# Nineteen seven-product blocks in place of eighteen, in another order, and two edits to the last block's tail

## The chip, the cores and the metric

The kernel runs on one core of a Trainium2 chip. A core has five engines that run side by side and meet through semaphores: TensorE (PE, matmuls, with its weight loads PEld), VectorE (DVE), ScalarE (ACT), GpSimd (POOL) and SyncE (SP). Each works through its own list of instructions in order. SP, ACT and POOL can also issue DMA transfers. The metric is the device time of one execution in microseconds, a median over runs.

## The reference

An input x of 8 x 4096 x 192 goes through a causal depthwise convolution over time with seven taps. Eight heads of 24 channels share a tap's weight, and the weights go through a softmax first. The result, as 32768 tokens of 192 channels, goes through a two-layer network: 192 to 2048, exact GELU, 2048 to 192.

```python
w = np.exp(weight - max); w = w / (w.sum(-1) + 1e-9)          # 8 heads x 7 taps
out = np.einsum('hk,bskhg->bshg', w, x_unf)                    # causal convolution
h = out.reshape(32768, 192) @ w_in                             # 192 -> 2048
g = 0.5 * h * (1 + erf(h / sqrt(2)))
return g @ w_out                                               # 2048 -> 192
```

## The kernel before

**Tiles.** The tokens are split in two halves of 16384, on 64 partitions each. A block n takes a run of tokens from both: blocks 0 to 5 take 256, blocks 6 to 34 take 512. While TensorE does the first product of block n, it does the second product of block n-1 in between.

**A block's way.** SP loads x into one of three buffers (`load`; a buffer is free when its last block is transposed). VectorE transposes it (`t`, line 1023). ScalarE writes the first tap as three scaled copies (`f0`, `f1`, `f2`, line 1157), VectorE adds the other six ("1" to "6", line 359; each tap waits for the one before; the sixth writes `xc`), POOL copies the six columns that overlap with the block before (`halo`). TensorE multiplies by w_in (line 1292, 48 rounds; a round is four 64x512 matmuls that run side by side), ScalarE applies GELU in 16 steps (line 1199) and writes `gT`, TensorE multiplies by w_out, the result is transposed into `osb` by VectorE and stored by SP (line 845, four DMAs a block).

**Two kinds of second product.** A plain block ("N") takes 48 rounds (line 1377) and three evacuations `ev.0` to `ev.2` by VectorE (line 477). A seven-product block (in `ST`) treats two of the three 64-channel thirds of the output as a 2x2 block product with seven products in place of eight, in Winograd's form: 44 rounds (line 1426). It pays in sums that other engines make of `gT`:

- `S1` in three parts (line 734) and `S3` in three parts: `S3.2` by VectorE (line 737), `S3.0` and `S3.1` by POOL as accumulating DMAs (line 691).
- `Dn` in two parts (line 740). Where the block before is plain, `Dn.0` is made by POOL instead, as a copying DMA (`cp`) and an accumulating one (lines 717, 721). Then `S4` in two parts (line 743).
- Four ScalarE copies out of PSUM, `p15`, `e`, `u`, `p3` (line 782); POOL moves u's result with two DMAs, `cu` and `cg` (line 686).
- VectorE's `k0` (line 790), which waits for the group P7 of the block's own matmuls and without which P4, later in the same block, can't start; `k3` (797), which waits for `cu`; `k4` (803), which waits for `cg` and for the block's last matmul; and three evacuations (line 815).

**The order.** It is written out by hand. `LIST[n]` is VectorE's order while it makes block n's convolution: a word `S1.0.8` is part 0 of S1 of block 8, `t9` is a transpose, a digit is a tap, `w` is one of ten preparations of the weights for the seven products, `evac` an evacuation of block 5. `SLOT[b]` tells before which GELU step of block b ScalarE does a first tap or a copy. `GLIST` is POOL's order. `AHEAD[n]` tells how many blocks SP has asked for before it stores block n-1. VectorE works about two blocks ahead of the GELU, so block m's sums stand in lists m+1 and m+2.

**The tail.** Block 34's second product runs alone, as 128x128 matmuls (line 1482) of four groups g of two banks h, 16 matmuls each. Group 0 of bank 0 waits for the GELU after every fourth. VectorE evacuates bank 0 of each group (line 449) and SP stores it, ScalarE evacuates bank 1 (line 451) and stores it (line 459). SP first stores all of block 33.

Of the kernel before, what the change touches and what calls it, by code (L numbers as in the profile page):

```python
# [11 lines left out]
def bass_lightweight_conv__then__act_gelu_exact_kernel(  # L12
# [24 lines left out]
    NB = len(WS)  # L37
# [16 lines left out]
    AHEAD = {4: 11, 5: 11, 7: 13, 8: 15, 9: 16, 10: 16, 11: 19, 12: 19, 13: 20, 14: 21, 15: 22, 16: 23, 17: 25, 18: 25, 19: 25, 22: 26, 23: 31, 24: 31, 25: 33, 26: 33, 27: 33, 28: 35, 29: 35}  # L54
# [20 lines left out]
    ST = [m for m in [8, 10, 11, 13, 14, 16, 17, 19, 20, 22, 24, 25, 27, 29, 30, 31, 32, 33] if m < M1]  # L75
    TYPE = {m: "S" if m in ST else "N" for m in range(-4, NB + 4)}
    LIST = {
        4: "t5 w.0.0 w.1.0 1 2 w.2.0 3 4 5 6",
        5: "t6 1 2 3 4 w.3.0 5 6",
        6: "w.4.0 t7 1 w.5.0 2 w.6.0 3 4 5 6",  # L80
        7: "t8 1 2 3 evac.0.5 w.7.0 4 5 6",
        8: "evac.1.5 t9 1 2 3 4 5 6",
        9: "ev.0.6 1 t10 2 ev.2.6 3 ev.1.6 4 5 w.8.0 6",
        10: "t11 1 2 S1.0.8 3 S1.1.8 ev.0.7 w.9.0 4 ev.1.7 S1.2.8 ev.2.7 Dn.1.8 S3.2.8 5 6",
        11: "S4.0.8 S4.1.8 k0.0.8 t12 1 2 3 ev.2.8 4 5 6",
        12: "t13 1 2 3 S1.0.10 4 ev.0.9 k4.0.8 k3.0.8 S1.1.10 5 ev.1.8 ev.0.8 ev.1.9 S1.2.10 S3.2.10 6",
        13: "Dn.1.10 S4.0.10 ev.2.9 1 S4.1.10 2 k0.0.10 3 4 S1.0.11 S1.1.11 Dn.0.11 ev.2.10 5 S1.2.11 Dn.1.11 S3.2.11 t14 6",
        14: "k4.0.10 t15 S4.0.11 S4.1.11 ev.0.10 k0.0.11 1 2 k3.0.10 3 ev.2.11 4 ev.1.10 5 6",
        15: "t16 1 2 S1.0.13 3 4 k3.0.11 ev.1.11 5 k4.0.11 S1.1.13 ev.0.12 ev.1.12 S1.2.13 ev.2.12 ev.0.11 Dn.1.13 S3.2.13 S4.0.13 S4.1.13 6",
        16: "t17 k0.0.13 1 S1.0.14 2 3 Dn.0.14 ev.2.13 S1.1.14 4 S1.2.14 S3.2.14 Dn.1.14 5 k4.0.13 ev.0.13 S4.0.14 S4.1.14 6",  # L90
        17: "k0.0.14 k3.0.13 t18 1 2 ev.2.14 3 4 ev.1.13 5 k4.0.14 6",
        18: "t19 ev.0.14 1 S1.0.16 2 ev.0.15 3 S1.1.16 4 k3.0.14 ev.1.15 ev.2.15 S1.2.16 ev.1.14 S3.2.16 Dn.1.16 5 S4.0.16 S4.1.16 6",
        19: "t20 k0.0.16 S1.0.17 1 2 ev.2.16 S1.1.17 3 4 S1.2.17 Dn.0.17 5 S3.2.17 k4.0.16 Dn.1.17 S4.0.17 S4.1.17 k0.0.17 k3.0.16 6",
        20: "1 t21 ev.2.17 ev.1.16 2 ev.0.16 3 4 5 6",
        21: "1 2 S1.0.19 t22 3 k4.0.17 ev.0.17 k3.0.17 ev.0.18 4 S1.1.19 S1.2.19 ev.1.18 S3.2.19 5 Dn.1.19 ev.2.18 6",
        22: "ev.1.17 S4.0.19 S4.1.19 k0.0.19 t23 1 S1.0.20 S1.1.20 ev.2.19 2 3 S1.2.20 4 S3.2.20 Dn.0.20 Dn.1.20 k4.0.19 S4.0.20 S4.1.20 k0.0.20 5 6",
        23: "1 t24 ev.2.20 k3.0.19 ev.0.19 ev.1.19 2 3 4 5 6",
        24: "S1.0.22 1 k3.0.20 ev.1.20 k4.0.20 ev.0.21 S1.1.22 t25 ev.0.20 2 ev.2.21 S1.2.22 ev.1.21 S4.0.22 Dn.1.22 S3.2.22 3 S4.1.22 4 k0.0.22 5 6",
        25: "t26 1 ev.2.22 2 3 4 5 6",
        26: "1 2 k4.0.22 t27 ev.0.23 3 ev.0.22 S1.0.24 4 S1.1.24 5 ev.1.23 S1.2.24 Dn.1.24 S3.2.24 k3.0.22 ev.2.23 ev.1.22 6",  # L100
        27: "S4.0.24 S4.1.24 k0.0.24 1 2 S1.0.25 Dn.0.25 S1.1.25 ev.2.24 3 4 S1.2.25 S3.2.25 t28 5 k4.0.24 Dn.1.25 S4.0.25 S4.1.25 k0.0.25 k3.0.24 6",
        28: "1 t29 2 ev.2.25 3 ev.0.24 ev.1.24 4 5 6",
        29: "1 2 S1.0.27 t30 3 S1.1.27 4 ev.0.26 k4.0.25 ev.1.26 S1.2.27 5 ev.2.26 k3.0.25 S3.2.27 ev.0.25 6",
        30: "ev.1.25 Dn.1.27 S4.0.27 S4.1.27 k0.0.27 t31 1 2 3 ev.2.27 4 5 6",
        31: "t32 1 k4.0.27 2 S1.0.29 3 4 5 ev.0.28 S1.1.29 k3.0.27 6",
        32: "S1.2.29 ev.2.28 ev.1.28 ev.1.27 S3.2.29 S4.0.29 ev.0.27 Dn.1.29 1 S4.1.29 k0.0.29 2 S1.0.30 3 t33 S1.1.30 ev.2.29 4 Dn.0.30 S1.2.30 S3.2.30 S4.0.30 5 Dn.1.30 k4.0.29 S4.1.30 k3.0.29 ev.1.29 k0.0.30 ev.0.29 6",
        33: "t34 S1.0.31 S1.1.31 1 ev.2.30 2 S1.2.31 Dn.0.31 Dn.1.31 S3.2.31 S4.0.31 S4.1.31 k4.0.30 3 4 k3.0.30 k0.0.31 5 6",
        34: "S1.0.32 S1.1.32 Dn.0.32 ev.2.31 1 ev.1.30 S1.2.32 S4.0.32 S3.2.32 ev.0.30 Dn.1.32 k4.0.31 2 S4.1.32 3 k0.0.32 4 5 S1.0.33 6",
        35: "ev.2.32 S1.1.33 S1.2.33 k3.0.31 Dn.0.33 ev.0.31 S4.0.33 S3.2.33 ev.1.31 k4.0.32 ev.0.32 k3.0.32 ev.1.32 Dn.1.33 S4.1.33 k0.0.33 ev.2.33 k4.0.33 ev.0.33 k3.0.33 ev.1.33",
# [3 lines left out]
        3: "0:f0.5 4:f1.5 5:f2.5 7:f0.6",  # L113
        4: "2:f1.6 5:f2.6 6:f0.7",
        5: "2:f1.7 6:f2.7",
        7: "0:f0.8 3:f1.8 3:f2.8 8:f0.9 9:f1.9 12:f2.9",
        8: "1:f0.10 5:f1.10 6:f2.10 10:f0.11 10:f1.11",
        9: "5:f2.11 7:p15.8 11:f0.12 14:e.8 15:f1.12",
        10: "0:u.8 2:p3.8 3:f2.12 5:f0.13 9:f1.13",
        11: "4:f2.13 6:p15.10 13:e.10",  # L120
        12: "0:p3.10 2:u.10 5:f0.14 6:p15.11 8:f1.14 9:f2.14 12:f0.15 13:e.11 15:f1.15",
        13: "0:u.11 2:p3.11 3:f2.15 7:f0.16 9:f1.16",
        14: "4:f2.16 6:p15.13 8:f0.17 11:f1.17 13:e.13",
        15: "0:p3.13 2:u.13 6:p15.14 10:f2.17 13:e.14 14:f0.18",
        16: "0:u.14 2:p3.14 4:f1.18 5:f2.18 9:f0.19 13:f1.19",
        17: "4:f2.19 6:p15.16 10:f0.20 10:f1.20 13:e.16",
        18: "0:p3.16 2:u.16 5:f2.20 6:p15.17 13:e.17 14:f0.21",
        19: "0:p3.17 3:f1.21 3:u.17 5:f2.21",
        20: "3:f0.22 6:p15.19 8:f1.22 10:f2.22 11:f0.23 13:e.19",
        21: "0:p3.19 2:u.19 6:p15.20 10:f1.23 10:f2.23 14:e.20 15:f0.24",  # L130
        22: "1:u.20 2:f1.24 3:p3.20 5:f2.24",
        23: "3:f0.25 6:p15.22 8:f1.25 11:f2.25 13:e.22 14:f0.26",
        24: "0:f1.26 2:u.22 3:p3.22 4:f2.26 12:f0.27",
        25: "0:f1.27 3:f2.27 6:p15.24 13:e.24",
        26: "0:p3.24 2:u.24 4:f0.28 6:p15.25 10:f1.28 10:f2.28 14:e.25 15:f0.29",
        27: "1:p3.25 3:u.25 5:f1.29 6:f2.29 12:f0.30",
        28: "1:f1.30 5:f2.30 7:p15.27 11:f0.31 13:e.27 14:f1.31",
        29: "0:u.27 1:f2.31 4:p3.27 7:f0.32",
        30: "1:f1.32 3:f2.32 7:p15.29 13:e.29",
        31: "0:p3.29 2:u.29 4:f0.33 6:p15.30 10:f1.33 10:f2.33 13:e.30 14:f0.34",  # L140
        32: "0:p3.30 2:u.30 6:p15.31 10:f1.34 10:f2.34 13:e.31",
        33: "0:p3.31 2:u.31 7:p15.32 14:e.32",
        34: "0:p3.32 2:u.32 7:p15.33 13:e.33 15:u.33",
# [57 lines left out]
    with es:  # L201
# [627 lines left out]
        def store(e, m):  # L829
# [13 lines left out]
            for q in range(4):  # L843

                e.dma_start(
                    ap(
                        outt,
                        ((q // 2) * HALF + OFF[m]) * C + (q % 2) * (C // 2),
                        [[C, 32], [32 * C, WS[m] // 32], [1, C // 2]],
                    ),  # L850
                    ap(
                        osb[m % 2],
                        32 * q * 8 * C,
                        [[8 * C, 32], [C // 2, WS[m] // 32], [1, C // 2]],
                    ),
                ).then_inc(S_OUT[m % 2], 16)

        GLIST = (
            "halo.10 cp.0.8 halo.11 S3.0.8 S3.1.8 Dn.0.8 cu.0.8 halo.12 halo.13 "
            "cg.0.8 cp.0.10 S3.0.10 Dn.0.10 S3.1.10 S3.0.11 S3.1.11 cg.0.10 cu.0.10 "  # L860
            "halo.14 halo.15 cg.0.11 cu.0.11 halo.16 cp.0.13 Dn.0.13 S3.0.13 S3.1.13 "
            "S3.0.14 S3.1.14 halo.17 cg.0.13 cu.0.13 cg.0.14 halo.18 halo.19 cp.0.16 "
            "cu.0.14 S3.0.16 Dn.0.16 S3.1.16 S3.0.17 S3.1.17 cg.0.16 cu.0.16 halo.20 "
            "halo.21 cp.0.19 cu.0.17 halo.22 cg.0.17 S3.0.19 Dn.0.19 S3.1.19 S3.0.20 "
            "S3.1.20 cg.0.19 halo.23 cu.0.19 cu.0.20 cp.0.22 halo.24 cg.0.20 S3.0.22 "
            "Dn.0.22 S3.1.22 halo.25 halo.26 cu.0.22 cg.0.22 cp.0.24 halo.27 S3.0.24 "
            "S3.1.24 Dn.0.24 S3.0.25 S3.1.25 cg.0.24 cu.0.24 halo.28 cg.0.25 halo.29 "
            "halo.30 cp.0.27 cu.0.25 S3.0.27 Dn.0.27 S3.1.27 cu.0.27 cg.0.27 halo.31 "
            "halo.32 cp.0.29 S3.0.29 Dn.0.29 S3.1.29 S3.0.30 halo.33 S3.1.30 cg.0.29 "
            "cu.0.29 S3.0.31 S3.1.31 cg.0.30 cu.0.30 S3.0.32 halo.34 S3.1.32 cg.0.31 "  # L870
            "cu.0.31 S3.0.33 S3.1.33 cg.0.32 cu.0.32 cg.0.33 cu.0.33 "
        )

        @block.gpsimd
        def _(g):
            def win_in(q, hf, sm):
                c0, pat = part(q)
# [667 lines left out]
```

## Time and profile before

| what | value |
|---|---|
| median of 3 runs | 666.78 us (666.04 to 667.2) |
| the profiled execution | 665.89 us, its span 664.2 us |
| TensorE busy, granted clock | 658.3 us (99%), 1.00 |
| VectorE busy | 619.1 us (93%) |
| ScalarE busy | 598.3 us (90%) |
| POOL busy | 106.7 us (16%) |
| first projection of block 34 starts | 629.94 us |
| last GELU ends | 651.6 us |

The span counts from the first to the last instruction of one execution. A row of the timeline gives start, duration, engine, line, operation, out<-in and count; a bracket at its end is the idle time of the engine before it, and what ended that. A row of the waits gives who waited for whom, the sum, how many times, and the longest.

### The profile page before, as it was taken

How to read it: one execution, taken by the hardware profiler on the slowest of the kernel's cores; microseconds unless marked ns; L12 is line 12 of the kernel's file. 1: busy time of each engine (PE TensorE's matmuls, PEld its weight loads, DVE VectorE, ACT ScalarE, POOL GpSimd, SP SyncE). 2: the span in 40 equal slices, each digit the busy share in tenths (PEclk: the TensorE clock that was granted, in tenths of full speed). 3: DMA queues.
4: the chain of work that ended last, by engine and by line, in shares of the span. 5: the costliest groups of instructions: out<-in, count | busy, mean ns of one | idle time of the engine just before them, and what ended most of it. 6: DMA issues, size and time to landing. Idle time of an engine off the chain costs nothing.

```text
span 664.2 us, 27974 instructions
## 1 busy us (share of the span) xinstructions
PE 658.3 (99%) x12792; PEld 505.6 (76%) x12792; DVE 619.1 (93%) x555; ACT 598.3 (90%) x707; POOL 106.7 (16%) x175
## 2 busy tenths in 40 slices
PE   8999999999999999999999999999999999999998
PEld 8999655576778988777878755767777888777887
DVE  6999879999999999999999999999999999999962
ACT  8899999898899899999989998988998988899883
POOL 7000430102010110202120102011212020111110
PEclk9999999999999999999999999999999999999999
DMA  9749493935673691677444348947545855352364
GB/s 156 163 95 181 74 156 82 218 64 116 150 146 80 141 206 25 164 168 150 94 116 114 65 106 207 200 108 168 113 106 120 177 117 126 66 113 49 86 142 112
DMA packets 146438, 83.66 MB, mean 126 GB/s; under 512 B 129936, under 2 KB 138192, under 8 KB 146320
## 3 DMA queue, kind: packets, MB, share of 16 engines
q1 hardware_dynamic: 129328, 49.42, 34.8%
q0 software_dynamic: 15872, 31.86, 23.7%
q8 instruction: 100, 1.64, 1.1%
q10 hardware_dynamic: 1120, 0.59, 0.3%
q14 instruction: 18, 0.15, 0.1%
HBM read 31.51 MB, written 25.17 MB: 85 GB/s over the span
## 4 chain that ended last, share of the span: by engine, by line
PE 96%; DMA 2%; ACT 1%; DVE 0%; issue 0%; POOL 0%; ACTq 0%; DVEq 0%
PE hp L1292 49%; PE ob L1426 25%; PE ob L1377 16%; PE ob L1332 5%; DMA win<-in_moe_w_in_dram 1%; PE hp L1482 1%; PE ob L1482 1%; DMA p5s<-u 1%; ACT gT L1199 0%; DMA wsb<-in_weight_dram 0%; DVE wcol L996 0%; POOL win L381 0%; DVE p5s L803 0%; POOL win L878 0%; POOL dg L901 0%
## 5 line engine op out<-in xcount | busy, mean ns | idle before, releaser
L1199 ACT ACTIVATE gT<-hp 128x1024 bf16<-128x1024 f32 x510 | 513.3, 1022 | 52.4 <-PE hp L1292 44.8
L1292 PE MATMUL hp<-xc,win 64*64 64x512 bf16 (+2 forms) x6036 | 438.6, 366 | 0.6 <-DVE win L381 0.5
L1292 PEld LDWEIGHTS hp<-xc,win 64*64 64x64 bf16 (+1 forms) x6036 | 241.8, 105 | 75.9 <-ACT gT L1199 7.3
L359 DVE SCALAR_TENSOR_TENSOR acc<-xT,wcol,acc 128x1536 f32<-128x1536 f32 (+1 forms) x165 | 282.0, 1709 | 8.3 <-ACT acc L1157 5.4
L1426 PE MATMUL ob<-gT,wot 64*64 64x512 bf16 x1152 | 219.1, 376 | 0.0
L1426 PE MATMUL ob<-gT,wst 64*64 64x512 bf16 (+2 forms) x1152 | 203.4, 323 | 0.5 <-DVE p5s L803 0.5
L1377 PE MATMUL ob<-gT,wot 64*64 64x512 bf16 x1920 | 135.8, 376 | 0.0
L1426 PE MATMUL ob<-s_S,wot 64*64 64x512 bf16 (+2 forms) x864 | 132.7, 305 | 0.0
L1426 PEld LDWEIGHTS ob<-gT,wst 64*64 64x64 bf16 x1152 | 98.8, 107 | 15.8 <-DVE p5s L803 1.3
L1377 PEld LDWEIGHTS ob<-gT,wot 64*64 64x64 bf16 x1920 | 71.0, 107 | 32.6
L1426 PEld LDWEIGHTS ob<-gT,wot 64*64 64x64 bf16 x1152 | 88.9, 107 | 8.6
L1426 PE MATMUL ob<-s_S,wst 64*64 64x512 bf16 x288 | 79.5, 376 | 0.0
L1426 PEld LDWEIGHTS ob<-s_S,wot 64*64 64x64 bf16 x864 | 68.8, 107 | 11.0 <-issue 0.3
L1157 ACT ACTIVATE acc<-xT,wcol 128x512 f32<-128x512 f32 (+1 forms) x93 | 64.6, 702 | 0.0
L1023 DVE STREAM_TRANSPOSE xT<-xin 128x1536 f32<-128x1536 f32 (+2 forms) x39 | 59.6, 1536 | 2.9 <-DMA xin<-in_x_dram 1.7
L691 POOL DMA_DIRECT2D gT<-gT x36 | 32.0, 907 | 186.3 <-DVE s_S L734 186.3
L1426 PE MATMUL ob<-s_Dn,wst 64*64 64x512 bf16 x216 | 61.0, 376 | 0.0
L359 DVE SCALAR_TENSOR_TENSOR xc<-xT,wcol,acc 128x1536 bf16<-128x1536 f32 (+1 forms) x33 | 56.5, 1713 | 0.6
L734 DVE TENSOR_TENSOR s_S<-gT 128x1024 bf16<-128x1024 bf16 (+1 forms) x54 | 45.7, 853 | 1.6 <-ACT gT L1199 1.6
L1332 PE MATMUL ob<-wout,gT 64*128 64x192 bf16 x768 | 42.0, 243 | 0.0
L1332 PEld LDWEIGHTS ob<-wout,gT 64*128 64x128 bf16 x768 | 35.1, 94 | 3.3
L1426 PEld LDWEIGHTS ob<-s_S,wst 64*64 64x64 bf16 x288 | 30.8, 107 | 4.4
(100 smaller groups left out, 423.6 us busy)
## 6 DMA issues: line engine op xcount, KB each, us to landing
out_dram<-osb SPq DMA_DIRECT2D x124, 192.0 KB, 3.4
xin<-in_x_dram SPq DMA_DIRECT2D x116, 192.0 KB, 4.5
gT<-gT POOLq DMA_DIRECT2D x18, 512.0 KB, 4.9
gT<-gT POOLq DMA_DIRECT2D x18, 256.0 KB, 4.6
dn<-gT POOLq DMA_DIRECT2D x6, 512.0 KB, 3.0
dn<-s_S POOLq DMA_DIRECT2D x6, 512.0 KB, 6.2
xin<-in_x_dram SPq DMA_DIRECT2D x18, 96.0 KB, 2.4
win<-in_moe_w_in_dram POOLq DMA_DIRECT2D x24, 64.0 KB, 3.3
```

What stands on the lines that cost most here:

```text
L359: return e.scalar_tensor_tensor(dst, src, wk, a, op0=ALU.mult, op1=ALU.add)
L691: e.dma_start(quad(m, 1, 0, k, k1 - k), quad(m, 0, 0, k, k1 - k), accum_op=ALU.add).then_inc(S_AD["S3.%d" % q], 16)
L734: ins = v.tensor_tensor(t("S1"), quad(m, 1, 0, k, n), quad(m, 1, 1, k, n), ALU.add)
L1023: v.transpose(out, src).then_inc(S_TR)
L1157: a.activation(out=acc[n % 2][:, p * TB : p * TB + w], in_=ap(xT[n % 2], p * XW + HX, [[NP * XW, 128], [1, w]]), func=AF.Copy, scale=wcol[ ...
L1199: a.activation(out=ap(gT[n % 2], (i % 2 * NF + i // 2) * TB if n in ST else i * c * 2 * w, dst), in_=ap(ob, 2 * TB, [[4 * TB, 128], *src[1 ...
L1292: ins = t.matmul(hbuf(u, slice(fo, fo + fw), o, w), ap(win, f1, [[NP * F, 64], [2, fw]]), xc[n % NXC][r, p * TB : p * TB + w], start=(p == ...
L1332: ins = t.matmul(bb[sub], gT[m % 2][r, c0 : c0 + 128], wout[r, CH[sub][i] * C : (CH[sub][i] + 1) * C], start=(ph == 0 and k == 0), stop=(p ...
L1377: ins = t.matmul(bank(BK[m][j], slice(64 * h, 64 * h + 64), w), ap(wot, 64 * hf * NF * C + CH[h][i] * C + 64 * j, [[NF * C, 64], [1, 64]]) ...
L1426: ins = t.matmul(bank(BK[m][bk], slice(64 * cg, 64 * cg + 64))[:, c0 : c0 + w], wt_, x, start=(e == mine[0]), stop=(e == mine[-1] or e in ...
L1482: ins = t.matmul(banks(m, g)[h], gT[m % 2][:, c0 : c0 + 128], wout[:, CH[h][i] * C : (CH[h][i] + 1) * C], start=(i == 0), stop=(i == NF - 1),)
```

## The change

- `ST` has 19 blocks in place of 18: 8, 9, 11, 12, 14, 15, ... in pairs with one plain block between them up to 27, and then 29 to 33 as before. The old list had single ones (8, 22, 27) among its pairs.
- `LIST`, `SLOT`, `GLIST` and `AHEAD` are written anew to match. Which parts of a block's sums go by DMA is told by the same rule as before.
- In block 34's group 0 the first 12 matmuls of both banks come ahead of the last four of either.
- SP stores two of block 33's four parts, ScalarE the other two, behind its second half-evacuation of block 34.

```diff
-    ST = [m for m in [8, 10, 11, 13, 14, 16, 17, 19, 20, 22, 24, 25, 27, 29, 30, 31, 32, 33] if m < M1]
+    ST = [m for m in [8, 9, 11, 12, 14, 15, 17, 18, 20, 21, 23, 24, 26, 27, 29, 30, 31, 32, 33] if m < M1]
...
-        4: "t5 w.0.0 w.1.0 1 2 w.2.0 3 4 5 6",
-        5: "t6 1 2 3 4 w.3.0 5 6",
-        6: "w.4.0 t7 1 w.5.0 2 w.6.0 3 4 5 6",
-        7: "t8 1 2 3 evac.0.5 w.7.0 4 5 6",
-        8: "evac.1.5 t9 1 2 3 4 5 6",
-        9: "ev.0.6 1 t10 2 ev.2.6 3 ev.1.6 4 5 w.8.0 6",
-        10: "t11 1 2 S1.0.8 3 S1.1.8 ev.0.7 w.9.0 4 ev.1.7 S1.2.8 ev.2.7 Dn.1.8 S3.2.8 5 6",
-        11: "S4.0.8 S4.1.8 k0.0.8 t12 1 2 3 ev.2.8 4 5 6",
+        4: "1 t5 2 3 4 5 6",
+        5: "1 t6 2 3 4 5 6",
+        6: "t7 1 2 3 4 5 6",
+        7: "t8 1 2 3 w.0.0 w.1.0 4 w.2.0 w.3.0 5 w.4.0 w.5.0 6",
+        8: "w.6.0 w.7.0 w.8.0 evac.0.5 evac.1.5 t9 1 2 3 4 5 6",
+        9: "1 2 t10 ev.0.6 ev.1.6 ev.2.6 3 4 5 6",
+        10: "w.9.0 t11 S1.0.8 1 ev.0.7 2 3 4 S1.1.8 5 S1.2.8 ev.1.7 S4.0.8 S3.2.8 ev.2.7 Dn.1.8 6",
+        11: "S4.1.8 t12 k0.0.8 S1.0.9 1 Dn.0.9 S1.1.9 2 S4.0.9 ev.2.8 3 S1.2.9 4 S3.2.9 5 k4.0.8 6",
...
-        34: "S1.0.32 S1.1.32 Dn.0.32 ev.2.31 1 ev.1.30 S1.2.32 S4.0.32 S3.2.32 ev.0.30 Dn.1.32 k4.0.31 2 S4.1.32 3 k0.0.32 4 5 S1.0.33 6",
-        35: "ev.2.32 S1.1.33 S1.2.33 k3.0.31 Dn.0.33 ev.0.31 S4.0.33 S3.2.33 ev.1.31 k4.0.32 ev.0.32 k3.0.32 ev.1.32 Dn.1.33 S4.1.33 k0.0.33 ev.2.33 k4.0.33 ev.0.33 k3.0.33 ev.1.33",
+        34: "S1.0.32 ev.2.31 1 S1.1.32 2 S1.2.32 3 Dn.0.32 S3.2.32 ev.0.30 k4.0.31 Dn.1.32 k3.0.30 S4.0.32 S4.1.32 ev.1.30 k0.0.32 4 S1.0.33 5 6",
+        35: "ev.2.32 ev.0.31 S1.1.33 S1.2.33 Dn.0.33 k3.0.31 S3.2.33 Dn.1.33 k4.0.32 ev.0.32 ev.1.31 k3.0.32 S4.0.33 S4.1.33 ev.1.32 k0.0.33 ev.2.33 k3.0.33 k4.0.33 ev.1.33 ev.0.33",
...
-        7: "0:f0.8 3:f1.8 3:f2.8 8:f0.9 9:f1.9 12:f2.9",
+        5: "1:f1.7 2:f2.7 6:f0.8",
+        7: "0:f1.8 2:f2.8 6:f0.9 10:f1.9 10:f2.9",
...
-            "cu.0.31 S3.0.33 S3.1.33 cg.0.32 cu.0.32 cg.0.33 cu.0.33 "
+            "cu.0.30 cg.0.31 cu.0.31 S3.0.33 S3.1.33 cg.0.32 cu.0.32 cu.0.33 cg.0.33 "
...
-        def store(e, m):
+        def store(e, m, parts=range(4)):
...
                 store_half(a, g, 1)
+                if g == 1:
+                    store(a, NB - 2, (2, 3))
...
-                for h in range(2):
-                    for i in range(NF):
+                cut = (0, NF - 4, NF) if g == 0 else (0, NF)
+                for i0, i1 in zip(cut, cut[1:]):
+                    for h in range(2):
+                        for i in range(i0, i1):
...
-                    ins.then_inc(S_MM2)
+                        if i1 == NF:
+                            ins.then_inc(S_MM2)
...
-                store(sp, n - 1)
+                store(sp, n - 1, range(4) if n < NB - 1 else (0, 1))
```

## The prediction

> **What bounds the kernel now.** I read four views, from wide to narrow. First the page: engine totals and the chain that ended last.
>
> ```profile
> PE 658.3 (99%) x12792; PEld 505.6 (76%) x12792; DVE 619.1 (93%) x555; ACT 598.3 (90%) x707; POOL 106.7 (16%) x175
> PE 96%; DMA 2%; ACT 1%; DVE 0%; issue 0%; POOL 0%; ACTq 0%; DVEq 0%
> ```
>
> TensorE carries the chain, so fewer matmuls should help. But VectorE's 93% is a mean over a slow start and a tail, so I asked for its busy time in the steady part (columns: stretch, length, PE, PEld, DVE, ACT, POOL, clock, DMA):
>
> ```profile
> 100.00:640.00 540.00, 539.50 (x10544) 403.86 (x10540) 527.94 (x450) 494.36 (x574) 77.46 (x113) 1.00 0.58 124
> ```
>
> VectorE has 12 us free in 540. It is a second bound, right behind TensorE. What it waits for between the end of block 10's convolution (133.4) and that of block 34's (629.3):
>
> ```profile
> DVE s_S L734 <- ACT gT L1199: 1.4, 3, 1.1
> DVE osb L477 <- PE ob L1377: 1.4, 2, 0.9
> DVE acc L359 <- ACT acc L1157: 1.1, 2, 0.7
> DVE p5s L803 <- DMA p5s<-u: 1.0, 1, 1.0
> DVE wtf L790 <- PE ob L1426: 0.4, 1, 0.4
> DVE osb L815 <- issue: 0.4, 1, 0.4
> DVE tq L790 <- PE ob L1426: 0.3, 1, 0.3
> ```
>
> That is 6.0 us, all there is for VectorE to give. The timeline bounds the stretch (first row: the instruction after block 10's last tap; last row: block 34's last tap) and prices a tap:
>
> ```profile
> 133.35 1.22 DVE L743 TENSOR_TENSOR s_S<-gT,s_Dn 128x2048 bf16<-128x2048 bf16 x1
> ...
> 325.41 1.77 DVE L359 SCALAR_TENSOR_TENSOR acc<-xT,wcol,acc 128x1536 f32<-128x1536 f32 x1
> 327.11 0.70 DVE L815 STREAM_TRANSPOSE osb<-p5s 128x512 f32<-128x512 f32 x1
> 327.74 5.48 DVE L359 SCALAR_TENSOR_TENSOR acc<-xT,wcol,acc 128x1536 f32<-128x1536 f32 x3
> 333.25 1.82 DVE L359 SCALAR_TENSOR_TENSOR xc<-xT,wcol,acc 128x1536 bf16<-128x1536 f32 x1
> ...
> 627.53 1.81 DVE L359 SCALAR_TENSOR_TENSOR xc<-xT,wcol,acc 128x1536 bf16<-128x1536 f32 x1
> ```
>
> Block 34's first projection matmul starts at 629.94, 0.60 after that last tap ends (629.34): there VectorE is nearly late. A tap with another instruction behind it takes 1.70 from start to start (325.41 to 327.11); three taps with their own successors behind them take 5.51 (327.74 to 333.25), 1.84 each. The tail:
>
> ```profile
> 649.97 1.16 PE L1482 MATMUL ob<-wout,gT 128*128 128x192 bf16 x12
> 651.64 1.82 PE L1482 MATMUL ob<-wout,gT 128*128 128x192 bf16 x20 [0.51 <-ACT gT L1199]
> 653.30 2.80 PE L1482 MATMUL hp<-wout,gT 128*128 128x192 bf16 x32
> ```
>
> TensorE has issued 12 matmuls of bank 0, then waits for the last GELU, and 20 are left: 4 of bank 0, 16 of bank 1.
>
> **The change, part by part.** *TensorE.* One more seven-product block takes 44 rounds (a round: four 64x512 matmuls side by side) in place of 48. Block 8's first projection starts at 104.28 and block 9's at 125.00, 96 rounds, so a round is 0.216 us and the saving 4 x 0.216 = 0.86. It is a gain only where TensorE is the bound.
>
> *VectorE in the stretch.* Counted in both programs' order, the new one has one S4 sum more there (spacing 1.15 from start to start), three Dn (3 x 1.15), S1 (1.16 + 2 x 0.64), S3 (0.60), k0, k3 and k4 (0.73 + 0.69 + 0.61); evacuations stay at 70. Together 9.7. Against it, taps followed by their own successor fall from 46 to 26 of 144. By the rows above one such pair costs 0.14; over all taps in the stretch the means are 1.84 and 1.75, and a tap that itself waited takes 0.03 more, so 20 x (0.09 + 0.03) = 2.4, of which I take 2.2 since not every pair frees both. Other waiting pairs (a sum behind its operand) fall from 12 to 7, at about 0.16: 0.8. Before, the stretch took 629.34 - 133.35 = 496.0, of which 6.0 were waits: 490.0 of work. After: 490.0 + 9.7 - 3.0 = 496.7 of work. So even if every wait went, VectorE would need 0.7 more than it took before.
>
> *How many waits stay.* 3.5 of the 6.0 (for GELU, for block N's matmuls, for P7 ahead of k0) arise where VectorE has run ahead of TensorE. From k0 of block 8 to k0 of block 33, by the same spacings, VectorE's work was 499.5 before, against 2332 rounds x 0.216 = 503.7 of TensorE: it ran 4 ahead and had to wait. It is 505.2 now against 2328 rounds = 502.9: it runs behind. So these should nearly vanish. The other 2.5 (first taps, a transfer into p5s, one unnamed) depend on ScalarE's slots and on POOL's order: I keep a third, 0.8. Bounds: none, and all 6.0.
>
> *The start.* Block 8's first two taps on ScalarE move one GELU earlier and one tap leaves their group: 1.02 + 0.66, less about 0.2 for the GELU's own wait, so VectorE's block 8 starts 1.5 earlier than 89.39. Against that S4.0 of block 8 comes ahead of the stretch (+1.15), w.8 leaves (-0.34), and S1.0 of block 8 must now wait some 0.4 for its GELU (115.5): the stretch starts 0.2 to 0.3 earlier; I take 0.2, bounds -0.5 and +0.3. The weight preparations w.0 to w.6, moved from lists 4 to 6 into 7 and 8, fill time in which VectorE waits anyway (51.44 busy of 60 between 40 and 100).
>
> *ScalarE.* The extra block adds p15, e, u and p3: 0.60 + 0.26 + 0.58 + 0.60 = 2.0, under the 46 us that it is idle between 100 and 640. Cover gone, it would delay a GELU, and then S1.
>
> *POOL.* One S3 pair and one cu/cg pair more, one cp/Dn.0 pair fewer, past the same halo copies: 77 busy of 540. *SP.* Loads are asked for earlier or later by a block; each still waits for its buffer's transpose. No load shows in the waits above, so zero, up to 1.7 (the one load wait at the start).
>
> *The tail.* In the new order bank 1's first 12 matmuls (12 x 0.083 = 1.0) run ahead of the last GELU's wait. TensorE stood from 650.97 to 651.64, so this hides 0.67; bank 0 and 1 together then end 0.67 earlier and everything behind them moves along. The last store leaves ScalarE's queue behind the last evacuation (661.42 + 0.33), so it moves too. ScalarE's two stores of block 33 (an issue of that line took 0.32 to 2.0 on SP, 0.54 in the median) wait there for block 33's last evacuation (656.44) and stand behind ScalarE's second half-evacuation and in front of the third, now due at 658.78 - 0.67 = 658.1: 656.5 + 2 x 0.54 = 657.6 is in time; at 0.9 each the third slips by 0.2, and the fourth, which ends the kernel 2.6 later, has room. Bounds 0.3 and 0.9. k3 ahead of k4 follows cu ahead of cg: zero.
>
> **Sum.** Block 34's convolution ends -0.2 + 0.7 + 0.8 = 1.3 later. 0.5 of the 0.60 slack absorbs part: its matmuls start 0.8 later. Tail -0.67. Net +0.1. The profiled execution took 665.89 (span 664.2 and 1.7 around it), 0.9 under the median of 666.78; I add the shift to the median: **666.9 us**.
>
> **A rule against the trace.** The rows show 1.70 and 1.84 for a tap by what follows it. The Trainium skill, VectorE: DVE Perf Modes, section The DRAIN you can't avoid, says in its own measurement that a semaphore between chained VectorE instructions costs nothing extra; by that, spreading the taps would save nothing. The trace disagrees by 0.14 a pair.
>
> **The rivals.**
> - *VectorE keeps half of its waits (slower).* Then the 3.0 stand in place of 0.8: 669.1; with all of them 672.1. For it: new waits can take the place of old ones, and each now counts in full, since TensorE waits for k0 and for the tap. Against: they need VectorE ahead. It passes +0.2% from about 2.0 us of waits.
> - *Spreading the taps saves nothing (slower).* The 3.0 come back: 669.9. Against: the two prices stand apart throughout the trace. The rule of the Trainium skill above would give this.
> - *VectorE is not the bound (faster).* TensorE keeps the full 0.86 and the tail 0.67: 665.2, and as low as 663.7 if its own old waits in the stretch (1.6 of weight loads, for line 803 of VectorE) go too. For it: VectorE's sum misses by only 1 us in 497. Against: the sum itself.
> - *The tail gives nothing*, because the last transfers, not TensorE, set the end: 667.6, inside "same".
>
> **How the numbers follow.** About 0.2%, 1.3 us, is what a measurement of this kernel can tell. Forecast and idle tail 0.50, all within 0.2%. Faster rival 0.20. Slower: half the waits 0.22, no saving by spreading 0.06, something in the loads 0.02. The range runs from the faster rival, 665.2, to the forecast with 2.5 us of waits, a late start (+0.5) and a tail of 0.4: 669.4.
>
> **What would show it.** Right: VectorE's idle between blocks 10 and 34 falls from 6 to about 1; TensorE gets small waits for VectorE (k0, S4, k4) of some 2 to 3 us in sum; the bank-0 group has 8 matmuls left after the last GELU; the granted clock stays 1.00. Wrong: VectorE's idle stays above 2, a first tap or a load shows among its waits, or the last tap of block 34 ends before 629.

## The result, and the profile after

The changed kernel takes 665.49 us (median of 19 runs, 664.78 to 667.27), the kernel before 666.92 on the same chip (19 runs, 665.42 to 668.02). The ratio is 0.9985, with a 95% interval of 0.9979 to 0.9991: about 1.0 us faster (the medians differ by 1.4; this text goes by the ratio). The forecast was 666.9, no change; the time lies in its range (665.2 to 669.4) but at the low end, and the interval excludes no change. The two profiled executions hide this: 665.79 us after (span 664.0) against 665.89 before (span 664.2).

The page of the changed kernel first: engine totals, and the chain that ended last, by engine.

```profile
PE 659.0 (99%) x12808; PEld 524.7 (79%) x12808; DVE 626.1 (94%) x567; ACT 599.2 (90%) x711; POOL 109.1 (16%) x177
PE 95%; issue 1%; DMA 1%; POOL 1%; DVE 0%; ACT 0%; POOLq 0%; DVEq 0%
```

VectorE has 7.0 us more to do and TensorE still carries the chain. The steady part (columns: stretch, length, PE, PEld, DVE, ACT, POOL, clock, DMA):

```profile
100.00:640.00 540.00, 539.13 (x10553) 420.55 (x10545) 531.81 (x458) 494.84 (x576) 75.33 (x114) 1.00 0.57 123
```

VectorE went from 527.94 to 531.81 of 540. What it waited for between block 10's convolution and block 34's:

```profile
DVE gsm L803 <- DMA gsm<-uu: 1.3, 1, 1.3
DVE s_S L734 <- PE ob L1428: 0.8, 2, 0.5
DVE s_S L734 <- ACT gT L1199: 0.6, 2, 0.4
```

The waits for plain blocks' matmuls (1.4) and for first taps (1.1) that the kernel before had are gone, those for GELU fell from 1.4 to 0.6; 2.7 us are left of 6.0, and the largest is new (a k4 behind its copy). The ends of the stretch, from VectorE's timeline (the row behind block 10's last tap; block 34's last tap):

```profile
132.62 1.21 DVE L743 TENSOR_TENSOR s_S<-gT,s_Dn 128x2048 bf16<-128x2048 bf16 x1
...
627.67 1.82 DVE L359 SCALAR_TENSOR_TENSOR xc<-xT,wcol,acc 128x1536 bf16<-128x1536 f32 x1
```

Block 34's convolution ends at 629.49, 0.15 later than before; the forecast had 1.3. TensorE's first weight load of block 34 and the load behind its projection:

```profile
629.60 0.39 PEld L1294 LDWEIGHTS hp<-xc,win 64*64 64x64 bf16 x12 [0.55 <-issue]
630.29 0.10 PEld L1428 LDWEIGHTS ob<-gT,wot 64*64 64x64 bf16 x1 [0.29 <-DVE osb L815]
```

The first stands 0.55 and starts 0.11 after that tap's end (the view names no releaser). The second waits for the evacuation that follows the tap. The tail, TensorE's timeline of block 34's banks:

```profile
650.11 2.81 PE L1486 MATMUL ob<-wout,gT 128*128 128x192 bf16 x32
```

All 32 matmuls of group 0, 16 of each bank, run in one piece; the 0.51 of waiting in bank 0 is gone.

To see where the time goes I cut each span at the starts of ScalarE's GELUs, from the timelines (us):

| program | to block 2's first GELU | to block 34's first | to the last GELU | to TensorE's end | to the span's end |
|---|---|---|---|---|---|
| before | 26.76 | 604.69 | 19.14 | 10.80 | 2.77 |
| before, second profile | 26.87 | 605.48 | 19.16 | 10.80 | 2.95 |
| old schedule, new bank order | 26.38 | 604.53 | 19.16 | 10.10 | 2.97 |
| old schedule, ScalarE's stores | 28.54 | 604.73 | 19.13 | 10.80 | 2.44 |
| changed | 26.25 | 604.55 | 19.83 | 10.21 | 3.18 |
| changed, second profile | 26.35 | 604.18 | 19.83 | 10.22 | 3.23 |
| new schedule, old tail | 26.32 | 604.21 | 19.81 | 10.80 | 2.41 |
| changed, sums first | 27.75 | 604.31 | 19.80 | 10.13 | 2.69 |

Two differences repeat in all eight: the new schedule loses 0.67 in block 34, and the new bank order gains 0.6 to 0.7 on TensorE's end. In the long middle the new schedule is 0.55 shorter in these eight (means 604.31 against 604.86). That is not shown to repeat: with the three profiles of each schedule from the levelled and the relieved kernels below, the means are 604.46 against 604.76, and the ranges overlap (604.10 to 605.25, 604.14 to 605.48). The start varies by 2 us among programs whose instructions up to there are the same on all five engines.

### The profile page after: what moved, and what is told of

Read it like the earlier page. It is cut to its first block, busy times and chain, and to the rows that moved or that the text cites. A ratio compares the mean times of both kernels' runs of the same rounds, so it can differ in the third digit from the quotient of the medians.

```text
span 664.0 us, 28045 instructions
## 1 busy us (share of the span) xinstructions
PE 659.0 (99%) x12808; PEld 524.7 (79%) x12808; DVE 626.1 (94%) x567; ACT 599.2 (90%) x711; POOL 109.1 (16%) x177
## 4 chain that ended last, share of the span: by engine, by line
PE 95%; issue 1%; DMA 1%; POOL 1%; DVE 0%; ACT 0%; POOLq 0%; DVEq 0%
PE hp L1294 49%; PE ob L1428 26%; PE ob L1379 14%; PE ob L1334 5%; PE ob L1486 1%; PE hp L1486 1%; DMA win<-in_moe_w_in_dram 1%; DMA gsm<-uu 1%; POOL win L878 0%; POOL gT L691 0%; PE ob L1237 0%; DVE s_S L734 0%; POOL xTb L374 0%; DVE gsm L803 0%; PE ob L1294 0%
## 5 line engine op out<-in xcount | busy, mean ns | idle before, releaser
L1294 PE MATMUL hp<-xc,win 64*64 64x512 bf16 (+2 forms) x6036 | 446.4, 366 | 0.2
L1294 PEld LDWEIGHTS hp<-xc,win 64*64 64x64 bf16 (+1 forms) x6036 | 254.5, 105 | 66.2 <-ACT gT L1199 5.7
L1428 PE MATMUL ob<-gT,wot 64*64 64x512 bf16 x1216 | 234.7, 376 | 0.0
L1428 PE MATMUL ob<-gT,wst 64*64 64x512 bf16 (+2 forms) x1216 | 214.8, 323 | 0.8 <-DVE gsm L803 0.8
L1428 PE MATMUL ob<-s_S,wot 64*64 64x384 bf16 (+2 forms) x912 | 139.1, 305 | 0.0
L1379 PE MATMUL ob<-gT,wot 64*64 64x512 bf16 x1728 | 124.9, 376 | 0.0
L1428 PEld LDWEIGHTS ob<-gT,wst 64*64 64x64 bf16 x1216 | 103.3, 107 | 15.0 <-DVE gsm L803 1.7
L1428 PEld LDWEIGHTS ob<-gT,wot 64*64 64x64 bf16 x1216 | 99.8, 107 | 11.3 <-DVE osb L815 0.7
L1379 PEld LDWEIGHTS ob<-gT,wot 64*64 64x64 bf16 x1728 | 69.9, 107 | 24.0
L1428 PE MATMUL ob<-s_S,wst 64*64 64x512 bf16 x304 | 84.3, 376 | 0.0
L1428 PE MATMUL ob<-s_Dn,wst 64*64 64x512 bf16 x232 | 65.4, 376 | 0.0
L743 DVE TENSOR_TENSOR s_S<-gT,s_Dn 128x2048 bf16<-128x2048 bf16 x29 | 34.5, 1210 | 0.3
```

What stands on the lines that cost most here:

```text
L743: ins = v.tensor_tensor(t("S4"), quad(m, 0, 1, k, n), t("Dn"), ALU.add)
L1294: ins = t.matmul(hbuf(u, slice(fo, fo + fw), o, w), ap(win, f1, [[NP * F, 64], [2, fw]]), xc[n % NXC][r, p * TB : p * TB + w], start=(p == ...
L1379: ins = t.matmul(bank(BK[m][j], slice(64 * h, 64 * h + 64), w), ap(wot, 64 * hf * NF * C + CH[h][i] * C + 64 * j, [[NF * C, 64], [1, 64]]) ...
L1428: ins = t.matmul(bank(BK[m][bk], slice(64 * cg, 64 * cg + 64))[:, c0 : c0 + w], wt_, x, start=(e == mine[0]), stop=(e == mine[-1] or e in ...
```

## The experiments

**The parts alone.** `schedule_only` is the changed kernel with the old tail, `banks_only` and `stores_only` are the kernel before with one tail edit each, `before_again` is the kernel before.

The first, against the changed kernel:

```diff
-                if g == 1:
-                    store(a, NB - 2, (2, 3))
...
-                cut = (0, NF - 4, NF) if g == 0 else (0, NF)
-                for i0, i1 in zip(cut, cut[1:]):
...
-                store(sp, n - 1, range(4) if n < NB - 1 else (0, 1))
+                store(sp, n - 1)
```

> The new schedule (blocks, lists, slots, POOL's order, look-ahead) with the old tail: bank 0 and bank 1 of block 34 one after the other, all stores of block 33 on SP. If VectorE is the bound, as forecast, it needs 1.3 us more up to block 34's last tap and the kernel is 0.8 us slower than before (ratio 1.0012). If TensorE is the bound and keeps its four rounds, it is 0.9 us faster (0.9987), and up to 1.6 faster if TensorE's old waits go too (0.9976).

> The kernel before, with only the order of block 34's first two banks changed. If TensorE sets the end, the 0.67 us in which it stood before the last GELU is hidden: 0.67 us faster (0.9990). If the last transfers set the end, as the two profiles suggest (TensorE ends 0.54 earlier in the new one, the last store lands only 0.13 earlier), 0.1 to 0.2 us faster (0.9998).

> The kernel before, with only two stores of block 33 issued by ScalarE. Forecast: no change (1.0000), at most 0.2 us slower through a late third half-evacuation. If the transfers at the end are the bound, spreading their issue over two queues could be worth up to 0.5 us either way (0.9993 to 1.0007).

> The kernel before, unchanged, profiled once more: what differs between two profiled executions of one program. If nothing but the end of the program varies, TensorE reaches block 34's first projection at 629.94 again, give or take 0.1; if the waits in the middle vary, it is off by up to 1 us, which is how far the first profiled execution lay under the median.

Measured: the schedule alone 0.9985 (0.9974 to 0.9996), the whole of the gain; the bank order alone 1.0002 (0.9991 to 1.0014); the stores alone 1.0000 (0.9990 to 1.0010). So the sign of the schedule was wrong, and the tail's 0.67 does not show in the times; the interval of the bank order, -0.6 to +0.9 us, only just excludes it. In the table it depends on the schedule. From the last GELU to the span's end the old one takes 13.57 and 13.75, and 13.07 with the new bank order: 0.5 to 0.7 sooner (13.10 for 13.65 with the start levelled, below). The new one takes 13.21 with the old tail, 13.39 and 13.45 with the whole new tail, stores included: TensorE's end comes 0.59 sooner there (10.21 for 10.80), and the span ends 0.77 later behind it (3.18 for 2.41). A DMA view of the kernel before by stretch fits a bound by transfers (columns as above; DMA share and GB/s last):

```profile
658.00:660.00 2.00, 2.00 (x28) 2.00 (x26) 0.00 (x0) 0.33 (x1) 0.00 (x0) 1.00 0.98 248
660.00:662.00 2.00, 1.39 (x17) 1.16 (x15) 0.36 (x1) 0.33 (x1) 0.00 (x0) 1.00 0.98 276
```

The 16 DMA engines are 98% busy from 658 to 662 in the kernel before, around TensorE's end at 661.4. The profiles of the old schedule show that the middle repeats to 0.02 us in most blocks; block 20 (20.46 or 21.10) and block 31 (19.95 to 20.80) vary most.

**Levelling the start.** If only the start differed by chance, taking it out should have shown it.

```diff
+            for s in S_WIN + S_WOUT:
+                t.wait_ge(s, 16)
+            t.wait_ge(S_XP, 64)
+            t.wait_ge(S_XIN[0], xin_at(3))
+            t.wait_ge(S_XIN[1], xin_at(4))
             p01 = [(1, kd, k) for k in taps for kd in (0, 1)]
```

> The kernel before, with its start levelled: TensorE begins block 0's first convolution only when all weights and the input of blocks 2 to 4 have landed (about 19 us), so that how late a weight lands no longer moves the program; some 10 us slower than before. All theories expect a narrower spread than the 2.6 us of before if the spread comes from the start.

> The changed kernel with the same levelled start; to be read against start_before. If the 1.0 us that the changed kernel gained lies in the first 26 us (its two profiles reach block 2's first GELU at 26.2 and 26.3, the four of the old schedule at 26.4 to 28.5), it is within 0.4 us of start_before. If it lies in the steady part (TensorE's four rounds, 0.86, and fewer waits), it is again about 1.0 us faster than start_before. By the forecast (VectorE is the bound, +0.8, and the tail -0.67), 0.1 slower.

> The levelled start with the new schedule and the old tail; against start_before. By the forecast 0.8 us slower; if TensorE is the bound in the steady part 0.9 us faster; by the profiles (block 2's first GELU to the last one takes 624.0 in the new schedule, 623.7 to 624.6 in the old) within 0.4.

> The levelled start with the old schedule and the new order of block 34's first two banks; against start_before. If TensorE sets the end, 0.67 us faster; if the last transfers do, within 0.2.

Measured: 685.26, 684.78, 685.54 and 684.58, each over 4 or 5 runs and spread over 1.0 to 2.9 us. It failed as a tool: the loads that it waits for vary by as much as the start did, and it cost 19 us in place of 10 (TensorE's clock was granted at 0.8 and then 0.5 to 0.6 in the first two of 40 slices). The differences of 0.3 to 0.7 decide nothing.

**VectorE relieved.** Two of seven taps were cut to a third in every block from 11 on; the convolution is incomplete in these two.

```diff
             w = WS[n]
+            if n >= 11 and k in (3, 4):
+                pn = 1
             kt = KS - 1 - k
```

> The kernel before with VectorE relieved: taps 3 and 4 of every block from 11 on run over the first third of their channels only (a third of the work left out, so the convolution is incomplete), some 2.4 us less VectorE work a block. If VectorE holds TensorE up in the stretch, TensorE falls to its own rounds: block 8's first GELU to block 34's in 524.1 (26 x 20.72 less 17 x 0.863) in place of 526.1 to 526.9, and the kernel is 2 to 3 us faster than before. If TensorE's losses have another cause, it is as fast as before.

> The changed kernel with the same relief, to be read against light_before. If VectorE is what holds TensorE up in both, the new schedule now shows its four rounds in full and the 0.66 us that block 34 takes longer up to its last GELU go as well: 3 to 3.5 us faster than before, 0.9 us faster than light_before, of which the end may take back some. If TensorE's losses have another cause, it is as fast as the changed kernel, 665.5.

Measured: 1.0001 (0.9986 to 1.0016) and 0.9979 (0.9969 to 0.9990), as their parents. Block 34's first GELU comes 605.01 and 604.11 after block 2's: no faster. The relieved changed kernel, in the same stretch of 133 to 629 (first its row, then that of the changed kernel):

```profile
133.00:629.00 496.00, 495.23 (x9737) 388.92 (x9731) 442.64 (x420) 455.20 (x533) 68.91 (x106) 1.00 0.58 125
```

```profile
133.00:629.00 496.00, 495.23 (x9725) 395.48 (x9719) 489.70 (x419) 455.23 (x532) 70.04 (x106) 1.00 0.58 125
```

47 us less of VectorE's work, and TensorE is at the same 495.23. VectorE only waits more, for GELU above all (its waits in the relieved kernel, 133 to 640):

```profile
DVE s_S L736 <- ACT gT L1201: 16.8, 16, 2.2
DVE gsm L805 <- DMA gsm<-uu: 7.3, 7, 3.4
DVE osb L479 <- PE ob L1381: 5.8, 4, 2.4
```

So VectorE's amount of work does not set the time of either kernel. The gap ahead of block 34 is no exception. In every profile of the new schedule, relieved or not, block 34's first GELU starts 1.32 after its last tap. The list puts S1.0 of block 33 ahead of taps 5 and 6, and that sum waits for a matmul of block 32's second product (the matmuls that still read the sum's buffer). It starts at the same time in the changed kernel and in the relieved one:

```profile
624.68 1.23 DVE L734 TENSOR_TENSOR s_S<-gT 128x2048 bf16<-128x2048 bf16 x1 [0.33 <-PE ob L1428]
```

```profile
624.58 1.22 DVE L736 TENSOR_TENSOR s_S<-gT 128x2048 bf16<-128x2048 bf16 x1 [1.75 <-PE ob L1430]
```

It is order, not volume.

**The sums of the last list first, and the changed kernel again.** The edit is a piece of `LIST[35]`:

```diff
-k4.0.32 ev.0.32 ev.1.31 k3.0.32 S4.0.33 S4.1.33 ev.1.32 k0.0.33 ev.2.33
+k4.0.32 ev.1.31 S4.0.33 S4.1.33 k0.0.33 ev.0.32 k3.0.32 ev.1.32 ev.2.33
```

> The changed kernel with one edit in the last list: block 33's S4 sums and k0 go ahead of three evacuations and one k3 of block 32 and behind one evacuation of block 31. In the changed kernel the last GELU starts 19.8 us after block 34's first, in the old schedule 19.1: if that 0.66 is TensorE waiting for these sums on VectorE, it goes, and the kernel is 0.3 to 0.7 us faster than the changed one (about 665.0). If the transfers at the end are the bound whatever TensorE does, no change.

> The changed kernel, unchanged, once more. In the four profiled executions with the old schedule block 2's first GELU starts at 26.4 to 28.5, in the two with the new one at 26.25 and 26.32. If the new schedule starts the program earlier for a reason of its own, it is again below 26.4; if how late a weight lands is chance, anything from 26.2 to 28.5. The time again some 1.0 us under before, if the first comparison was no chance.

Measured: 0.9981 (0.9970 to 0.9993) and 0.9988 (0.9976 to 0.9999). k0 of block 33 comes 2.0 us sooner, and the last GELU still starts 19.80 after block 34's first: the 0.67 there is not these sums. Two of the changed kernel's waits remain as its place: the 0.29 above, in front of a load that stands behind the matmuls of block 34's first GELU, and 0.43 for an S3 transfer. Together they are 0.72. (The 0.55 lies ahead of that GELU and is no part of the 0.67.) The start went to 27.75 in one of the two and 26.35 in the other: the new schedule does not start earlier by itself.

**Time taken off TensorE.** 160 matmuls of the first projection were left out (40 rounds, in blocks 14 to 23; the output is incomplete).

```diff
+                if 14 <= n <= 23 and 2 <= i <= 5:
+                    todo = [q for q in todo if q[1] != 1]
                 for cc, p in todo:
```

> The kernel before with 40 rounds (160 matmuls of the middle contraction part, four rounds in each of blocks 14 to 23) left out of the first projection, so its output is incomplete: 40 x 0.216 = 8.6 us less for TensorE. If TensorE alone sets the end, 8.6 us faster, 658.2. By the forecast VectorE stands right behind, with 6 us of waits to give: 6 us faster at most, 660.8.

> The changed kernel with the same 40 rounds left out. If TensorE alone sets the end, 8.6 us faster than the changed kernel, 656.9. If VectorE stands right behind (2.7 us of waits left in the stretch, and block 34's first projection 0.14 behind its last tap), only some 3 us faster, 662.5.

Measured: 663.48 (0.9952, 0.9940 to 0.9964), 3.1 us faster, and 668.75 (1.0028, 1.0017 to 1.0038), slower than the changed kernel by 2.9 us going by the ratios, with 8.6 us less to do. Neither theory has the second. The ten blocks themselves, from block 14's first GELU to block 24's (changed kernel, then with the rounds left out):

```profile
226.89:429.12 202.23, 202.23 (x3943) 158.07 (x3939) 200.91 (x169) 185.97 (x218) 29.88 (x47) 1.00 0.62 135
```

```profile
226.97:428.97 202.00, 198.13 (x3783) 134.95 (x3778) 200.68 (x169) 185.35 (x217) 29.84 (x47) 1.00 0.62 135
```

They take 202.00 in place of 202.23, with VectorE busy for 200.68 of it and ScalarE for 185.35: there VectorE holds TensorE up. In the old schedule the same ten blocks fall from 201.86 to 199.33. What TensorE's weight loads then wait for (changed kernel with rounds left out, 133 to 655; the first item is 4.8 in the changed kernel):

```profile
PEld hp L1296 <- ACT gT L1199: 10.9, 38, 0.8
PEld ob L1430 <- DVE gsm L803: 4.3, 5, 1.4
PEld ob L1430 <- DMA gT<-gT: 3.1, 2, 1.8
PEld ob L1430 <- DVE s_S L734: 2.0, 3, 1.2
PEld ob L1430 <- issue: 1.9, 4, 0.9
```

VectorE then needs 497.7 for the stretch, 2.9 of it waits. So in the new schedule TensorE and VectorE end within about a microsecond of each other, while the old one had 3 us to spare. Relieving either alone gained nothing there. That it becomes slower rather than equal lies elsewhere: block 34 takes 21.21 up to the last GELU and TensorE's tail 11.69, for 19.83 and 10.21. In each, TensorE is late by one of POOL's transfers (an S3 sum, then a `cg`), whose last part lands 1.4 and 1.8 us behind the other fifteen, with an instruction fetch (a 16 KB transfer that brings a piece of TensorE's program) running across it. In the changed kernel no fetch crosses these two transfers, and they land whole. The 160 matmuls and their weight loads are also 20 KB of program, so the edit moves every later fetch; the next group is about that.

**Instruction fetches.** In block 10 the new schedule has a wait that the old one lacks (VectorE, then TensorE's weight loads, changed kernel):

```profile
152.75 0.69 DVE L803 TENSOR_TENSOR gsm<-ob,gsm 128x512 f32<-128x512 f32 x1 [1.25 <-DMA gsm<-uu]
```

```profile
153.50 0.11 PEld L1428 LDWEIGHTS ob<-gT,wst 64*64 64x64 bf16 x2 [1.25 <-DVE gsm L803]
```

The copy was issued at 148.57. Fifteen of its sixteen parts landed by 150.76, the last at 152.66. A 16 KB instruction fetch ran from 150.5 to 151.4. The next kernels lengthen TensorE's program ahead of block 10, so that fetches fall elsewhere: `shift` by 8 KB in the warm-up, `pad` by 13 KB of idle waits in blocks 6 and 7.

```diff
-            for i in range(48):
-                t.matmul(hp[1][:, 0:128], one, one)
+            for i in range(112):
+                t.matmul(hp[1][0:32, 0:32], one[:, 0:32], one[:, 0:32])
...
             def mm1(n, i):
                 w, c = WS[n], NCH[n]
+                for _ in range({6: 14, 7: 12}.get(n, 0)):
+                    t.wait_ge(S_WSB, 16)
```

> The kernel before, with the 48 warm-up matmuls of 128x128 at the start replaced by 112 of 32x32, which makes TensorE's program 128 instructions (8 KB, half of a 16 KB instruction fetch) longer ahead of everything else. If instruction fetches that meet a transfer make the waits that come and go in block 20 (0.66) and 31 (up to 0.85), their places change; the time by less than 1 us either way. If the place of the program in memory has no effect, same as before.

> The changed kernel with the same shift by half a fetch. In the three profiles of the new schedule whose transfer I followed, 15 of 16 parts of the copy that k4 of block 8 waits for land 2.2 us after its issue and the last one 1.3 to 1.9 us later, with a 16 KB instruction fetch at 149.8 to 150.5 across it. If the fetch is the cause, it now runs some 3 us off, the last part lands with the others, and block 10 takes 20.2 in place of 20.7 to 21.0: 0.5 to 0.8 us faster there. If the copy is late for another reason, block 10 stays at 20.7 to 21.0.

> The changed kernel with 208 idle instructions (13 KB, waits on a semaphore that is long there) spread over TensorE's program in blocks 6 and 7, so that the start is untouched and every later instruction fetch comes some 5 us earlier against the work, that is about 1 us later than the one before it came. The fetch at 150.5 then comes at about 151.6, behind the copy that lands at 150.8: block 10 takes 20.0 to 20.2 in place of 20.6 to 21.0, and the kernel is 0.5 to 1 us faster than the changed one (about 664.8), unless another transfer is met that TensorE waits for.

> The kernel before with the same 208 idle instructions. No sign is forecast: if fetches that meet transfers decide about a microsecond or more, its time moves by another amount than that of pad_after, and the difference between the two schedules is neither the 1.1 us of the unshifted pair nor the 2.9 of the pair shifted by 8 KB. If they do not, the difference is 1.1 again.

The fetch moved to 147.4 (shift) and 152.0 (pad), and block 10, which took 20.4 to 21.0 in every other profile of the new schedule, takes 20.0 in both. In `shift` the fetch is over 1.0 us before the copy is issued (at 149.75). In `pad` the copy comes later too (issued at 150.16), and the fetch still begins 0.4 before the fifteenth part lands, yet the sixteenth lands with it. The copy's row in the DMA view (148 to 154), changed kernel first with its fetch from queue 8, then the shifted one, where that row is gone:

```profile
q8 instruction: 1, 0.02, 1.0%
...
gsm<-uu POOLq DMA_DIRECT2D x1, 128.0 KB, 4.1
```

```profile
gsm<-uu POOLq DMA_DIRECT2D x1, 128.0 KB, 2.2
```

With the fetch out of the way the late part is gone; `pad` shows that a fetch across a copy does not always bring one. The times, however, rose:

| TensorE's program | old schedule | new schedule | difference |
|---|---|---|---|
| as it was | 666.92 | 665.49 | -1.4 (by the ratio -1.0) |
| 8 KB longer | 670.37 (1.0054, 1.0042 to 1.0066) | 667.45 (1.0012, 1.0002 to 1.0022) | -2.9 |
| 13 KB longer, in blocks 6 and 7 | 668.62 (1.0026, 1.0011 to 1.0042) | 668.72 (1.0026, 1.0016 to 1.0036) | +0.1 |

The idle waits were not free (blocks 2 to 7 took 1.1 to 1.4 more in the profiles), but that is alike in both. Shifted by 8 KB, the old schedule's middle takes 607.44, with new waits in blocks 15, 23, 25, 26 and 33; the new one's takes 603.78, but its block 34 20.93 for 19.83. About 1 us of the shift's cost lies in the start (27.99 and 27.43 to block 2's first GELU). The shift also replaces the warm-up's matmuls, but TensorE's first convolution starts at 5.8 as before, so whether that part is the place or chance is open. In `pad` with the new schedule TensorE's tail takes 11.41 for 10.21, behind a copy whose last part is 1.6 late with a fetch across it. The difference between the schedules goes from nothing to 2.9 us with the place of the program. No version clearly beats the changed kernel.

## Why the prediction was wrong

- *VectorE's work in the stretch, 496.7: a term mis-sized.* It was 494.2, with 2.1 to 2.7 of waits in place of 0.8: 496.3 to 496.9 in all for the forecast 497.5. The counts of what was added held (9.7 at the old prices). The saving by the other order was 5.5, not 3.0: a tap fell from 1.783 to 1.760 from start to start (144 taps: 3.4, forecast 2.2), and the input transpositions, S1, Dn, k3 and k4 got 0.01 to 0.03 cheaper each (S4 0.01 dearer), where only 0.8 had been allowed. Rows from one order priced the work in another 2.5 us, or 0.5%, too high.
- *From there to "its matmuls start 0.8 later": the step that failed.* The sum let VectorE's work alone say when block 34 starts, and gave TensorE's 0.86 nothing before it. With 47 us less of VectorE's work both kernels take the same time, so it is not what sets that start; VectorE stands right behind TensorE (within about 1 us, by the rounds left out) but did not pass it. The schedule alone came out 1.0 us faster in place of 0.8 slower. In the profiles the convolution's end, counted from block 2's first GELU, came 0.2 later (603.0 against 602.8 in four profiles each), not 1.3, and block 34's first GELU 0.55 sooner (0.3 over seven profiles each), not 0.8 later. This is the rival "VectorE is not the bound", at its price of 665.2 nearly the measured 665.49, though not by its mechanism: it was to keep all of 0.86 and the tail.
- *TensorE's 0.86.* Some 0.3 to 0.55 of it is left in the middle, less than two profiles of one schedule differ there (up to 1.3); block 10's new wait, which no step had, takes part of it.
- *The slack of 0.60 at block 34.* It was used up as forecast, but the wait there came from the list's order. The two waits that follow cost block 34 0.67 that was not in the sum.
- *The tail, -0.67.* Right on TensorE (0.59 to 0.70 in the profiles). At the end the bank order alone measured 1.0002, as the rival "the tail gives nothing" had it, though its profile ends 0.5 to 0.7 sooner behind the last GELU, so what reaches the end is open. The rival's reason, transfers, fits the DMA rows; that was not tested by taking transfers away. The forecast's +0.1 was a sum of +0.8 for the schedule and -0.67 for the tail, and neither showed in the times.
- *ScalarE's two stores, POOL, SP at zero.* Stores alone 1.0000. Of POOL's edits the copy of block 8 was not free.
- *The rival "spreading saves nothing".* Refuted, but at a smaller price than the forecast's. Over the stretch a tap with another tap right behind it takes 1.83 from start to start before and 1.81 after, one with something else behind it 1.76 and 1.74: a pair costs 0.07, not the 0.14 of the two rows. Twenty pairs fewer are 1.4 of the taps' 3.4. The rest is that both kinds got 0.01 to 0.02 shorter, and no run shows why. The Trainium skill, VectorE: DVE Perf Modes, section The DRAIN you can't avoid, says that a semaphore between chained VectorE instructions costs nothing extra. Its measurement has copies with and without a semaphore; these rows have another instruction in between, so they do not contradict it, and the prediction's "the trace disagrees" goes too far.
- *What should have shown it.* TensorE's small waits for VectorE came (2.6 in sum, 1.7 of them for k4), the bank order showed as said, the clock stayed at 1.00. VectorE's idle was 2.1 to 2.7, above the 2 that was to show the forecast wrong.

What stays open: behind block 2's first GELU the profiles give the changed kernel -0.3 us against before (637.4 and 638.4 before, 637.8 and 637.5 after), less than two profiles of one kernel differ, while the times over 19 runs each give -1.0. The start may hold the rest (mean 27.1 for the four programs of the old schedule in the table, 26.7 for the new), but the programs are the same up to there, and levelling it did not decide. With a schedule's worth moving from 0 to 2.9 us by the program's place, -1.0 is the worth of this edit at this place of the program, not of the edit anywhere.

## What to carry to other kernels

When two engines end within a microsecond in 600, price neither by the other's rows alone: relieve each one on its own and see whether the end moves. Read a saving at the end from the last store, not from the last matmul, where the DMA engines are 98% busy there. For an edit worth less than about 3 us here, also measure both kernels with the long engine's program shifted by some kilobytes, since 8 KB more of program moved one of them by 3.8 us and the other by about 2. If an edit takes instructions out, it moves the program too.

## What the runs showed that was not expected

- The last part of a transfer can land late when an instruction fetch runs across it. Over the 20 profiles I took `cu` and `cg`, the copies of u's result, and called one late when the last of its sixteen parts landed more than 0.5 us behind the fifteenth. Of 464 that a 16 KB fetch crossed (it ran between the issue and the fifteenth landing) 188 were late; of 276 without a fetch, 2. So a fetch across the copy goes with nearly every late part, but most crossings do no harm; what decides is open. POOL's other copies were late more often with a fetch as well (498 of 807, against 59 of 273). The Trainium skill, Advanced Engine Details and Errata, section ISA Cache, gives lines of 16 KB for 256 instructions; the packets in the trace are of that size.
- A shift of TensorE's program by 8 KB, with the work behind the warm-up the same, cost the kernel before 3.8 us (0.5%).
- Leaving out 8.6 us of TensorE's work, and with it 20 KB of program, made the changed kernel about 3 us slower.
- TensorE's middle part repeats to 0.02 us in most blocks from one execution to the next. The places that vary by half a microsecond or more are few (blocks 20 and 31 of the old schedule; 10 and 28 of the new, and once block 7).
